# Lightning attention and mixture of depths: the first ten groups as one chunk of 128 tokens, and expert pieces between the halves of the later groups

## The chip, the cores and the metric

The kernel runs on one core of a Trainium2 chip. Time is device time in microseconds (us) of one execution of the whole program. The engines are named as in the profile: PE (TensorE, the matrix engine), DVE (VectorE), ACT (ScalarE), POOL (GpSimd) and SP (SyncE, which here only issues transfers). A fp32 matmul is two matmul instructions with a weight load each (a transpose is one), so 16 matmuls of the code are x32 in the profile.

## The reference

Two steps with four batches of 768 tokens, 8 heads of 64 and, joined, 512 features. The first is linear attention with a decay `lam` per head; it walks over blocks with a running state. Any block length gives the same result up to rounding.

```python
for b in range(nb):                       # blocks of 64 tokens
    intra = einsum('bhic,bhjc->bhij', qb, kb) * Dmask      # Dmask[i, j] = lam**(i-j), i >= j
    intra = einsum('bhij,bhjd->bhid', intra, vb)
    inter = einsum('bhid,bhde->bhie', qb * lam_pow, kv_state)
    out[:, :, sl] = intra + inter
    kv_state = lam**block * kv_state + einsum('bhsd,bhse->bhde', kb * rev_pow, vb)
```

The second is a mixture of depths: each batch's 128 tokens with the highest gate score go through a small network, and the result is added to their rows.

```python
scores = einsum('bsd,d->bs', x, w_gate)
for b in range(B):
    top_idx = argpartition(-scores[b], capacity)[:capacity]        # 128 of 768
    xe = x[b, top_idx]
    ye = maximum(xe @ w1, 0.0) @ w2                                # 512 -> 1024 -> 512
    out[b, top_idx] = xe + sigmoid(scores[b, top_idx])[:, None] * ye
```

## The kernel before, in words

The work is cut into 24 groups `g` of 128 tokens, all 8 heads, six groups to a batch. One loop over `g` runs from -1 to 23, and its order is written out by hand: the program's order on each engine is the order of the calls. Iteration `g` prepares group `g+1` and finishes group `g`.

A group is computed as two chunks of 64 tokens, `c = 0, 1`, with states `n = 2g + c`. Heads come in pairs: `hp` is the pair, `hh` the head in it. Every product is a 64x64 quarter of the array (`quarters()` lists 16 of them), placed on rows and columns 0 to 63 or 64 to 127.

- `transposes(g, name)`: q or k, four 128x128 transposes into a PSUM bank (`m` in the profile; four banks go round), copied to SBUF by ACT as `qT` or `kT`.
- `queries_decayed(g)`: POOL multiplies `qT` by powers of lam, giving `qs`. `keys_decayed(g)`: `kd`, by ACT in eight instructions for the first nine groups, then by POOL in one.
- `state_products(g)`: `kd` times v, into the right half of the PSUM tile `su`; `next_state(n)`: DVE adds the decayed state to it; `decay_state(n)`: POOL decays a state. So a group has the chain state, decay, state, decay over DVE and POOL.
- `scores(g)`: k times q into the left half of `su`; `masked(g)`: DVE multiplies by the decay mask, giving `p`.
- `from_states(g)`: `qs` times the two states, into the PSUM tile `o_`; `from_scores(g)`: `p` times v, added to it. Between them `settle(g)`, a tiny DVE copy `seen` that reads `o_`, so that the second waits until the first has arrived.
- `outputs(g)`: ACT copies `o_` to the output tile `x_b` in three instructions; `store(g)`: SP writes it to DRAM; `gate_scores(g)`: DVE's product `xg` of `x_b` with the gate weights, summed to a score per token.

The ranks follow a few groups later: `row(g)` (PE transposes the scores, ACT copies them), `compare(g)` (DVE compares every score with all of its batch, giving `beat`, `table`, `ranks`), `column_sums(g)` (PE sums the tables, DVE subtracts), and after a batch's last group `find(b)` (DVE, six `hit` instructions), `tokens(b)` (PE, with two DVE steps) and `fetch(b)` (POOL's indirect transfer of the 128 chosen rows; `take` is both). The network of a batch is 17 pieces: `gate` (four transposes of the rows), eight `hidden` (eight instructions of 128x128 each), eight `back` (two of 128x512). `products(n)` runs the next `n` pieces. `flush()` runs what goes after: `weigh` and `finish` (DVE's `y`, then POOL's indirect write).

SP's queue holds the loads and the stores in the order of the calls: three loads of 256 KB for one group, then the store of the group before. `AHEAD` is the number of load buffers, `ahead(g)` how many groups ahead loads are asked for (4 at first); from iteration `W0` on, the network's weights are loaded.

In iterations before `START = 9` the loop has no pieces: transposes of `g+1`, `row` and sums, `from_states(g)`, `settle(g)`, `gate_scores(g-1)`, `compare(g-2)`, `state_products(g+1)`, `from_scores(g)`, `scores(g+1)`, `outputs(g)`, the two states, `masked(g+1)`. From 9 on, three pieces with the rank work stand ahead of the transposes; then the rest follows in the same order, with `gate_scores(g)` at the end.

Of the kernel before, what the change touches and what calls it, by code (L numbers as in the profile page):

```python
# [17 lines left out]
def kernel(  # L18
# [29 lines left out]
    AHEAD = 10  # L48
    W0 = 9
    START = 9  # L50
# [52 lines left out]
    ident2 = const.tile([128, C], FP32, name="ident2")  # L103
    nc.vector.tensor_tensor(out=ident2[:], in0=ident[:, :C], in1=ident[:, C:], op=ALU.add)
    zero = const.tile([128, C], FP32, name="zero")
    nc.vector.memset(zero[:], 0.0)

    mask = const.tile([128, 2, NHP, C], FP32, name="mask")
    for hh in range(2):
        for hp in range(NHP):  # L110
            h = 2 * hp + hh
            nc.vector.tensor_tensor_scan(
                out=mask[:, hh, hp, :], data0=lam_b[:, h : h + 1].broadcast_to([128, C]),
                data1=ident2[:], initial=0.0, op0=ALU.mult, op1=ALU.add,
            )
    kpow = const.tile([128, NHP, 2], FP32, name="kpow")
    nc.vector.tensor_copy(kpow[:].rearrange("p a b -> p b a"), mask[:, :, :, C - 1])
# [3 lines left out]
    qpow = const.tile([128, NHP, 2, C], FP32, name="qpow")  # L121
    for hp in range(NHP):
        for c in range(2):
            nc.vector.tensor_tensor_scan(
                out=qpow[:, hp, c, :], data0=lam_p[:, hp : hp + 1].broadcast_to([128, C]),
                data1=zero[:], initial=1.0, op0=ALU.mult, op1=ALU.add,
            )
    decay = const.tile([128, NHP, D], FP32, name="decay")
    nc.vector.tensor_copy(decay[:], qpow[:, :, 0, C - 1 : C].broadcast_to([128, NHP, D]))
# [14 lines left out]
    states, decayed = {}, {}  # L144
# [6 lines left out]

    def keys_decayed(g):
        if g >= NG:
            return
        kd = att.tile([128, H, D], FP32, name="kd", bufs=2)
        if g < START:
            for h in range(H):
                nc.scalar.activation(  # L158
                    kd[:, h, :], loaded[g][0][:, h, :], AF.Copy,
                    scale=kpow[:, h // 2, h % 2 : h % 2 + 1],  # L160
                )
            kds[g] = kd
            return
        nc.gpsimd.tensor_tensor(  # L164
            out=kd[:], in0=loaded[g][0][:],
            in1=kpow[:].rearrange("p a b -> p (a b)").unsqueeze(2).broadcast_to([128, H, D]),
            op=ALU.mult,
        )
        kds[g] = kd
# [14 lines left out]
    def queries_decayed(g):  # L184
        if g >= NG:
            return
        qs = att.tile([128, NHP, L], FP32, name="qs")
        nc.gpsimd.tensor_tensor(  # L188
            out=qs[:], in0=qTs[g][:], in1=qpow[:].rearrange("p a c i -> p a (c i)"), op=ALU.mult
        )  # L190
        qss[g] = qs

    def scores(g):
        if g >= NG:
            return
        qT, kT = qTs.pop(g), kTs.pop(g)
        for hp, hh, c in quarters():
# [5 lines left out]
    def masked(g):  # L203
        if g >= NG:
            return
        p = att.tile([128, 2, NHP, C], FP32, name="p")
        nc.vector.tensor_tensor(
            out=p[:].rearrange("p a b i -> p a (b i)"), in0=su[:, :, : NHP * C],
# [4 lines left out]
    def state_products(g):  # L213
        if g >= NG:
            return
        vn, kd = loaded[g][2], kds.pop(g)
        for hp, hh, c in quarters():
# [9 lines left out]
    def decay_state(n):  # L227
        if n // 2 >= NG or n % (2 * NT) == 0 or n % (2 * NT) == 2 * NT - 1:
            return
        t = att.tile([128, NHP, D], FP32, name="decayed", bufs=2)  # L230
        nc.gpsimd.tensor_tensor(out=t[:], in0=states[n][:], in1=decay[:], op=ALU.mult)  # L231
        decayed[n] = t

    def next_state(n):
        if n // 2 >= NG or n % (2 * NT) == 2 * NT - 1:
            return
        new = att.tile([128, NHP, D], FP32, name="state", bufs=8)
        u = su[:, n % 2, NHP * C :].rearrange("p (b e) -> p b e", e=D)
# [4 lines left out]
        states[n + 1] = new  # L243

    def from_states(g):
        qs = qss.pop(g)
        for hp, hh, c in quarters():
# [11 lines left out]
    def from_scores(g):  # L259
        p, vn = ps_.pop(g), loaded.pop(g)[2]  # L260
        for hp, hh, c in quarters():
            nc.tensor.matmul(  # L262
                o_[half[hh ^ c], hh, hp * D : (hp + 1) * D],
                lhsT=p[half[c], hh, hp, :], rhs=vn[half[c], 2 * hp + hh, :],
# [12 lines left out]
    def outputs(g):  # L277
# [4 lines left out]
        x_b = x_bs[b]  # L282
        po = [o_[:, hh, : NHP * D].rearrange("p (b e) -> p b e", e=D) for hh in range(2)]
# [11 lines left out]
    def gate_scores(g):  # L295
        b, t = divmod(g, NT)
        xg = mod.tile([128, HD], FP32, name="xg")
        nc.vector.tensor_tensor_reduce(  # L298
# [191 lines left out]

    def constants():
        nc.gpsimd.memset(lead[:], TINY)
# [52 lines left out]
    def early(g):  # L545
        return g < START

    def second(g):
        next_state(2 * g + 1)
        decay_state(2 * g + 2)  # L550

    for g in range(-1, NG):
# [5 lines left out]
        if early(g):  # L558
            transposes(g + 1, "qT")
            transposes(g + 1, "kT")  # L560
            if NGR:
                row(g - 2)
                column_sums(g - 3)
        else:
            products(1)
            if NGR:
                column_sums(g - 3)
                row(g - 2)
                if ends(g - 4) and (g - 4) // NT > 0:
                    take((g - 4) // NT)  # L570
                compare(g - 2)
                if ends(g - 3):
                    find((g - 3) // NT)
            products(1 + (not ends(g - 6)))
            if ends(g - 6):
                for i in range(NGR):
                    pieces.extend(expert((g - 6) // NT, i))
                products(1)
            transposes(g + 1, "qT")
# [83 lines left out]
```

## Time and profile before

| | us |
|---|---|
| runs, median of 3 | 204.72 (204.28 to 207.6) |
| profiled execution | 202.72 |
| its span, first to last instruction | 200.9 |
| PE busy | 157.3 (78%), 3580 matmul instructions |
| DVE, POOL, ACT busy | 103.7, 90.1, 88.0 |
| mean granted clock of TensorE | 0.955 |

The durations below are of the profiled execution; 1.8 us of its time lie outside of the span, and the median of the runs is 2.0 above it. Busy time is that of an engine's instructions; a matmul's end is modelled. "Idle before" is the time that an engine stood still ahead of a group of instructions, with the instruction that released it; "issue" there means that nothing in the profile released it. The granted clock is the share of 2.4 GHz; its lower level is 1.2 GHz, 0.5.

### The profile page before, as it was taken

The page shows a single profiled execution, that of the slowest core. Times are in us where ns is not written, and L with a number is a line of the kernel's source. Part 1 is how long each engine was busy: PE and PEld are TensorE (multiplying, and loading weights), DVE is VectorE, ACT ScalarE, POOL GpSimd, SP SyncE. Part 2 cuts the span into 40 slices and gives each one's busy share as a digit, 9 for nine tenths or more (in the row PEclk, how much of TensorE's full clock was granted, in tenths as well). Part 3 has the DMA queues.
Part 4 walks back from the last instruction along what each step waited for, and adds up shares of the span by engine and source line. Part 5 has one row for each costly group of instructions (what it writes and reads, how often), then busy time and mean ns, then how long its engine had stood idle before and what let it go on. Part 6 is the DMA issues. An engine that isn't in the chain of part 4 may idle for free.

```text
span 200.9 us, 8297 instructions
## 1 busy us (share of the span) xinstructions
PE 157.3 (78%) x3580; PEld 129.4 (64%) x3580; DVE 103.7 (52%) x376; ACT 88.0 (44%) x257; POOL 90.1 (45%) x99
## 2 busy tenths in 40 slices
PE   0597765973977768795969995998999859998990
PEld 0496655962975657695836774998666649748730
DVE  2636663763678676575435658274766566001001
ACT  0968887696452443453324352354424441103200
POOL 3165555053585956357337837355596120102001
PEclk9999997999798899999999999799999996999999
DMA  3999999599688989999989998911022120101001
GB/s 107 229 224 247 247 226 206 116 224 218 129 186 196 324 194 295 253 242 263 300 197 250 260 224 190 264 64 54 7 68 92 55 77 33 52 0 55 0 0 52
DMA packets 82500, 32.26 MB, mean 161 GB/s; under 512 B 75680, under 2 KB 77728, under 8 KB 82464
## 3 DMA queue, kind: packets, MB, share of 16 engines
q1 hardware_dynamic: 81536, 29.37, 62.1%
q0 software_dynamic: 640, 2.10, 3.0%
q8 instruction: 28, 0.46, 1.0%
q10 hardware_dynamic: 288, 0.27, 0.4%
q14 instruction: 8, 0.07, 0.1%
HBM read 24.38 MB, written 7.34 MB: 158 GB/s over the span
## 4 chain that ended last, share of the span: by engine, by line
PE 49%; issue 18%; DVE 14%; POOL 8%; DMA 5%; ACT 3%; POOLq 1%; SPq 0%; DVEq 0%; ACTq 0%
PE m L450 11%; PE m L177 10%; PE m L462 7%; PE o L251 5%; PE o L262 5%; PE su L198 5%; PE su L221 5%; DVE xg L298 4%; POOL decayed L231 4%; POOL qs L188 3%; DMA qn<-in_q_dram 3%; DVE state L242 2%; DMA out_dram<-y,tok 2%; DVE y L475 1%; DVE table L339 1%
## 5 line engine op out<-in xcount | busy, mean ns | idle before, releaser
L231 POOL TENSOR_TENSOR decayed<-state,decay 128x256 f32<-128x256 f32 x40 | 34.5, 863 | 33.1 <-DVE state L242 26.9
L188 POOL TENSOR_TENSOR qs<-qT,qpow 128x512 f32<-128x512 f32 x24 | 31.1, 1294 | 34.0 <-ACT qT L181 34.0
L450 PE MATMUL m<-xsT,w_sb 128*128 128x128 f32 x256 | 36.1, 296 | 9.1 <-DVE y L475 3.8
L450 PEld LDWEIGHTS m<-xsT,w_sb 128*128 128x128 f32 x256 | 33.0, 206 | 10.5 <-DVE y L475 4.1
L242 DVE TENSOR_TENSOR state<-su,decayed 128x256 f32<-128x256 f32 x40 | 17.0, 425 | 30.8 <-PE su L198 20.8
L462 PE MATMUL m<-w_sb,hs 128*128 128x512 f32 x64 | 30.6, 605 | 0.0
L298 DVE CUSTOM_DVE_ANT_0 xg<-x_b,wg_b 128x512 f32<-128x512 f32 x24 | 25.0, 1040 | 2.0 <-ACT x_b L286 2.0
L177 PE MATMUL m<-ident,qn 128*128 128x128 f32 x96 | 17.0, 306 | 10.0 <-DMA qn<-in_q_dram 7.3
L198 PE MATMUL su<-qT,kT 64*64 64x64 f32 x768 | 17.8, 227 | 7.0 <-issue 6.9
L284 ACT COPY x_b<-o 128x256 f32<-128x256 f32 x24 | 8.9, 373 | 31.5 <-PE o L262 31.5
L251 PE MATMUL o<-state,qs 64*64 64x64 f32 x704 | 18.7, 235 | 4.5 <-issue 4.5
L177 PEld LDWEIGHTS m<-ident,qn 128*128 128x128 f32 x96 | 12.2, 155 | 14.5 <-issue 12.1
L181 ACT COPY qT<-m 128x512 f32<-128x512 f32 x24 | 14.0, 582 | 15.6 <-PE m L177 15.6
L251 PEld LDWEIGHTS o<-state,qs 64*64 64x64 f32 x704 | 14.9, 143 | 8.2 <-issue 7.7
L198 PEld LDWEIGHTS su<-qT,kT 64*64 64x64 f32 x768 | 15.2, 142 | 7.7 <-issue 7.4
L221 PE MATMUL su<-vn,kd 64*64 64x64 f32 x704 | 18.5, 231 | 1.8 <-POOL kd L164 1.7
L454 ACT ACTIVATE hs<-m 128x128 f32<-128x128 f32 x32 | 8.9, 277 | 24.3 <-PE m L450 24.2
L262 PE MATMUL o<-vn,p 64*64 64x64 f32 x768 | 17.3, 228 | 2.4 <-DVE seen L272 2.4
L479 POOL DMA_INDIRECT out_dram<-y,tok x4 | 4.6, 1158 | 30.6 <-DVE y L475 30.6
L158 ACT ACTIVATE kd<-kn,kpow 128x64 f32<-128x64 f32 x72 | 18.2, 335 | 0.2
L286 ACT COPY x_b<-o 64x256 f32<-64x256 f32 x48 | 17.6, 367 | 0.6
L221 PEld LDWEIGHTS su<-vn,kd 64*64 64x64 f32 x704 | 16.0, 145 | 2.7 <-POOL kd L164 2.0
(61 smaller groups left out, 207.5 us busy)
## 6 DMA issues: line engine op xcount, KB each, us to landing
kn<-in_k_dram SPq DMA_DIRECT2D x24, 256.0 KB, 4.5
qn<-in_q_dram SPq DMA_DIRECT2D x24, 256.0 KB, 5.2
vn<-in_v_dram SPq DMA_DIRECT2D x24, 256.0 KB, 5.6
out_dram<-x_b SPq DMA_DIRECT2D x24, 256.0 KB, 3.6
w_sb<-in_moe_w_dram SPq DMA_DIRECT2D x8, 512.0 KB, 5.5
wg_b<-in_moe_w_gate_dram ACTq DMA_DIRECT2D x1, 256.0 KB, 4.7
xs<-out_dram,tok POOLq DMA_INDIRECT x4, 4.2
out_dram<-y,tok POOLq DMA_INDIRECT x4, 3.4
```

The lines of the kernel that those rows point to most:

```text
L158: nc.scalar.activation(kd[:, h, :], loaded[g][0][:, h, :], AF.Copy, scale=kpow[:, h // 2, h % 2 : h % 2 + 1],)
L177: nc.tensor.transpose(tp[:, hp * L : (hp + 1) * L], in_=t[:, 2 * hp : 2 * hp + 2, :], identity=ident[:])
L188: nc.gpsimd.tensor_tensor(out=qs[:], in0=qTs[g][:], in1=qpow[:].rearrange("p a c i -> p a (c i)"), op=ALU.mult)
L198: nc.tensor.matmul(su[half[c], hh, hp * C : (hp + 1) * C], lhsT=kT[half[hh], hp, half[c]], rhs=qT[half[hh], hp, half[c]], start=True, stop ...
L221: nc.tensor.matmul(su[half[hh], c, NHP * C + hp * D : NHP * C + (hp + 1) * D], lhsT=kd[half[c], h, :], rhs=vn[half[c], h, :], start=True, ...
L231: nc.gpsimd.tensor_tensor(out=t[:], in0=states[n][:], in1=decay[:], op=ALU.mult)
L242: nc.vector.tensor_tensor(out=new[:], in0=u, in1=decayed.pop(n)[:], op=ALU.add)
L251: nc.tensor.matmul(o_[half[hh ^ c], hh, hp * D : (hp + 1) * D], lhsT=qs[half[hh], hp, half[c]], rhs=states[n][half[hh], hp, :], start=(hp ...
L262: nc.tensor.matmul(o_[half[hh ^ c], hh, hp * D : (hp + 1) * D], lhsT=p[half[c], hh, hp, :], rhs=vn[half[c], 2 * hp + hh, :], start=(hp == ...
L298: nc.vector.tensor_tensor_reduce(out=xg[:], in0=x_bs[b][:, t].rearrange("p a b e -> p (a b e)"), in1=wg_b[:], scale=1.0, scalar=0.0, op0=A ...
L450: nc.tensor.matmul(ph, lhsT=w1_sb[:, dc, f * 128 : (f + 1) * 128], rhs=keep["xsT"][:, dc, :], start=(dc == 0), stop=(dc == NDC - 1),)
L462: nc.tensor.matmul(py[:], lhsT=keep["hs"][:, f, :], rhs=w2_sb[:, f, :], start=(f == 0), stop=(f == NFC - 1),)
```

## The change

The first ten groups (`WIDE = 10`) are computed as one chunk of 128 tokens: `scores` is eight matmuls with 128 columns of weights and 128 moving columns, `from_states` eight with 128 columns of weights over half of the rows, `from_scores` eight with 128x128 weights and 64 moving columns, `state_products` eight over all rows. A group has one state and one decay instead of two. The state products go to a bank of their own, the scores fill all of `su`, the mask product is one of 1024 columns, `x_b` is copied by ACT in one instruction, the gate score reads `o_` in PSUM with a reordered copy of the gate weights (`wg_o`), `settle` is gone, and the keys of all groups are decayed by POOL. The constants are made for 128 tokens; `narrow_constants` takes those for 64 from them.

In the wide iterations `row(g-1)`, `compare(g-1)` and `column_sums(g-2)` come one group earlier than before, and `from_states(g+1)` stands in the iteration of group `g`, after `scores(g+1)`. In the later iterations the transposes come first, then `from_states(g)`, `settle(g)`, `state_products(g+1)` and the first state; then the pieces with the rank work and the second state; then `from_scores(g)`, `scores(g+1)`, outputs and mask. A batch's pieces begin at `ends(g - 5)` instead of `ends(g - 6)`. `AHEAD` is 8 instead of 10, and `W0` 8 instead of 9.

```diff
-    AHEAD = 10
-    W0 = 9
-    START = 9
+    AHEAD = 8
+    W0 = 8
+    WIDE = 10
...
     def scores(g):
         if g >= NG:
             return
         qT, kT = qTs.pop(g), kTs.pop(g)
+        if wide(g):
+            for hp in range(NHP):
+                for hh in range(2):
+                    nc.tensor.matmul(
+                        su[:, hh, hp * L : (hp + 1) * L], lhsT=kT[half[hh], hp, :],
+                        rhs=qT[half[hh], hp, :], start=True, stop=True, skip_group_check=True,
+                    )
+            return
         for hp, hh, c in quarters():
...
+                    nc.tensor.matmul(
+                        ub[half[hh], hp * D : (hp + 1) * D], lhsT=kd[:, h, :], rhs=vn[:, h, :],
+                        start=True, stop=True, skip_group_check=True,
+                    )
...
+                        nc.tensor.matmul(
+                            o_[:, hh, hp * D : (hp + 1) * D], lhsT=qs[half[hh], hp, :],
+                            rhs=states[2 * g][half[hh], hp, :],
+                            start=(hp == 0), stop=False, skip_group_check=True,
+                        )
...
+                    nc.tensor.matmul(
+                        o_[:, hh, hp * D : (hp + 1) * D], lhsT=p[:, hh, hp * L : (hp + 1) * L],
+                        rhs=vn[:, 2 * hp + hh, :], start=(hp == 0 and g % NT == 0), stop=True,
+                        skip_group_check=True,
+                    )
...
+        if wide(g):
+            nc.vector.tensor_tensor_reduce(
+                out=xg[:].rearrange("p (a m) -> p a m", a=2), in0=o_[:, :, : NHP * D],
+                in1=wg_o[:].rearrange("p (a m) -> p a m", a=2),
...
-        if early(g):
+        if wide(g):
+            if NGR:
+                if ends(g - 3):
+                    take((g - 3) // NT)
+                row(g - 1)
+                compare(g - 1)
+                column_sums(g - 2)
             transposes(g + 1, "qT")
             transposes(g + 1, "kT")
+            queries_decayed(g + 1)
+            if g >= 0:
+                from_scores(g)
+                outputs(g)
+                store(g)
+                gate_scores(g)
+            state_products(g + 1)
+            scores(g + 1)
+            if wide(g + 1):
+                from_states(g + 1)
...
+            next_state(2 * g + 2)
+            decay_state(2 * g + (3 if not wide(g + 1) else 4))
+            masked(g + 1)
+            second(g + 1)
+            if g == 1:
+                narrow_constants()
+            if NGR and ends(g - 2):
+                find((g - 2) // NT)
         else:
+            transposes(g + 1, "qT")
+            transposes(g + 1, "kT")
+            from_states(g)
+            settle(g)
+            queries_decayed(g + 1)
+            state_products(g + 1)
+            next_state(2 * g + 2)
+            decay_state(2 * g + 3)
+            keys_decayed(g + 2)
+            if ends(g - 5):
+                for i in range(NGR):
+                    pieces.extend(expert((g - 5) // NT, i))
             products(1)
             if NGR:
+                column_sums(g - 2)
...
+                    take((g - 3) // NT)
+                row(g - 1)
+            products(1)
+            second(g + 1)
+            if NGR:
+                compare(g - 1)
+                if ends(g - 2):
+                    find((g - 2) // NT)
+            products(1)
             from_scores(g)
+            scores(g + 1)
             outputs(g)
             store(g)
+            masked(g + 1)
             gate_scores(g)
+            flush()
```

How the instructions then stand, at three places. First PE in iteration 2, an early group, before the change (`m` is a PSUM bank, `sc` the scores of the tokens; L177 is `transposes`, L318 `row`, L251 `from_states`, L221 `state_products`, L262 `from_scores`, L198 `scores`):

```order
L177 MATMUL m_137<-ident,qn 128x128 x4
L177 MATMUL m_138<-ident,kn 128x128 x4
L318 MATMUL m_135<-ident,sc 128x128
L251 MATMUL o<-state,qs 64x64 x16
L221 MATMUL su<-vn,kd 64x64 x16
L262 MATMUL o<-vn,p 64x64 x16
L198 MATMUL su<-qT,kT 64x64 x16
```

And PE in iteration 1 of the changed kernel, from its `row` on (L401 `row`, L180 `transposes`, L324 `from_scores`, L248 `state_products`, L208 `scores`, L300 `from_states`):

```order
L401 MATMUL m_134<-ident,sc 128x128
L180 MATMUL m_135<-ident,qn 128x128 x4
L180 MATMUL m_132<-ident,kn 128x128 x4
L324 MATMUL o<-vn,p 128x64 x8
L248 MATMUL m_133<-vn,kd 64x64 x8
L208 MATMUL su<-qT,kT 128x128 x8
L300 MATMUL o<-state,qs 128x64 x8
```

64 matmuls of a quarter have become 32 wider ones, and `from_states` has moved behind `scores`, for the next group.

Second, DVE in the wide iteration 7 of the changed kernel, with what each instruction waits for (L374 is `gate_scores` with its accumulator, L289 `next_state`, L224 `masked`, L457 `find`, L472 and L474 `tokens`, L413 and L422 `compare`):

```order
L374 ISA xg,sc<-o,wg_o 128x512 [waits Activation_49]
L374 ISA sc 128x1
L289 TENSOR_TENSOR state<-m_133,decayed 128x256 [waits PE_49,Pool_49]
L224 TENSOR_TENSOR p<-su,mask_w 128x1024 [waits PE_49]
L457 TENSOR_SCALAR hit,found<-slot,ranks 128x128 [waits DVE_49]
L457 TENSOR_SCALAR hit,found<-slot,ranks 128x128 x5
L472 COPY two<-m_134 128x2 [waits PE_49]
L474 SCALAR_TENSOR_TENSOR tok_0_790<-two 128x1
```

The gate score now stands in the iteration of its own group, reads `o` and waits for ACT; `hit` stands between the mask and the token numbers.

Third, PE in a late group before the change, from the last two pieces ahead of iteration 17's transposes to two pieces of iteration 18 (L462 is `back`, L356 `column_sums`):

```order
L462 MATMUL m_138<-w_sb,hs 128x512 x2
L177 MATMUL m_136<-ident,qn 128x128 x4
L177 MATMUL m_137<-ident,kn 128x128 x4
L251 MATMUL o<-state,qs 64x64 x16
L221 MATMUL su<-vn,kd 64x64 x16
L262 MATMUL o<-vn,p 64x64 x16
L198 MATMUL su<-qT,kT 64x64 x16
L462 MATMUL m_138<-w_sb,hs 128x512
L356 LDWEIGHTS table
L356 MATMUL m_135<-ones,table 128x1
L318 MATMUL m_136<-ident,sc 128x128
L462 MATMUL m_138<-w_sb,hs 128x512 x2
```

And PE in a late iteration of the changed kernel (L311 `from_states`, L257 `state_products`, L545 `back`, L439 `column_sums`, L401 `row`, L331 `from_scores`, L214 `scores`):

```order
L180 MATMUL m_135<-ident,qn 128x128 x4
L180 MATMUL m_132<-ident,kn 128x128 x4
L311 MATMUL o<-state,qs 64x64 x16
L257 MATMUL su<-vn,kd 64x64 x16
L545 MATMUL m_134<-w_sb,hs 128x512
L439 LDWEIGHTS table
L439 MATMUL m_133<-ones,table 128x1
L401 MATMUL m_135<-ident,sc 128x128
L545 MATMUL m_134<-w_sb,hs 128x512
L331 MATMUL o<-vn,p 64x64 x16
L214 MATMUL su<-qT,kT 64x64 x16
```

The pieces and the rank work have moved from ahead of the transposes to between `state_products` and `from_scores`.

## Rows read from the trace of the kernel before

**Rows 1.** Windows by stage: length, busy us (instructions) by engine, granted clock, DMA share, GB/s

```profile
15.70:67.00 51.30, 37.20 (x1220) 33.70 (x1219) 30.83 (x109) 34.53 (x109) 26.51 (x28) 0.90 0.91 201
67.00:162.00 95.00, 80.84 (x1994) 65.99 (x1992) 56.88 (x198) 39.19 (x104) 53.58 (x52) 0.98 0.72 186
162.00:200.90 38.90, 30.88 (x173) 22.06 (x172) 9.33 (x40) 5.70 (x22) 4.37 (x4) 0.94 0.10 34
```

**Rows 2.** Timeline: start, length, engine, line, operation, tiles, idle before

```profile
15.69 1.19 SPq L290 DMA_DIRECT2D out_dram<-x_b  x1
...
67.03 0.36 SPq L290 DMA_DIRECT2D out_dram<-x_b  x1
...
161.31 0.74 ACT L286 COPY x_b<-o 64x256 f32<-64x256 f32 x2
...
171.41 0.96 POOL L408 DMA_INDIRECT xs<-out_dram,tok  x1 [6.45 <-DVE tok L391]
...
180.17 0.60 PE L421 MATMUL m<-ident,xs 128*128 128x128 f32 x4
```

**Rows 3.** Waits of PE in S1, 15.7 to 67: total, times, longest

```profile
PE o L251 <- issue: 4.5, 3, 1.7
PE su L198 <- issue: 4.2, 2, 3.3
PE m L177 <- issue: 2.5, 1, 2.5
```

**Rows 4.** Chain of work that ended last, 14 to 20 us

```profile
14.46 0.47 PE su L198 x32
14.93 1.03 PE m L177 x8
...
16.45 1.51 issue
...
18.87 0.55 PE o L262 x32
```

**Rows 5.** Windows between three gaps of PE, columns as in rows 1

```profile
17.90:22.50 4.60, 3.43 (x127) 3.05 (x127) 2.96 (x6) 3.72 (x13) 2.72 (x3) 1.00 1.11 266
22.70:27.50 4.80, 3.38 (x127) 3.00 (x127) 3.45 (x9) 4.15 (x15) 2.31 (x3) 1.00 1.02 228
```

**Rows 6.** DMA queues of the whole run: packets, MB, share of 16 engines

```profile
q8 instruction: 28, 0.46, 1.0%
```

**Rows 7.** Chain of work that ended last, 160 us to the end

```profile
162.09 0.69 DVE xg L298
...
162.79 0.66 DVE y L475
...
170.68 2.79 PE m L450 x24
173.46 6.88 PE m L462 x16
```

**Rows 8.** Groups of instructions: shape, count, busy us, mean ns, idle before

```profile
L207 DVE TENSOR_TENSOR p<-su,mask 128x512 f32<-128x512 f32 x24 | 16.3, 681 | 0.0
...
L181 ACT COPY qT<-m 128x512 f32<-128x512 f32 x24 | 14.0, 582 | 15.6 <-PE m L177 15.6
...
L374 DVE TENSOR_SCALAR_CACHE_REDUCE hit<-slot,ranks 128x128 bf16<-128x128 f32 x24 | 6.7, 341 | 0.0
```

**Rows 9.** Waits of PE in S2, 67 to 162

```profile
PE su L198 <- issue: 2.7, 2, 2.0
PE o L262 <- DVE seen L272: 2.4, 2, 1.8
PE m L450 <- issue: 2.3, 1, 2.3
PE m L450 <- DVE y L475: 2.3, 1, 2.3
```

**Rows 10.** DMA issues: median us from issue to landing

```profile
xs<-out_dram,tok POOLq DMA_INDIRECT x4, 4.2
```

More of the change, by code (lines that the diff above doesn't have):

```diff
@@ L143 @@
     qTs, qss, kTs, kds, ps_ = {}, {}, {}, {}, {}
-    states, decayed = {}, {}
+    states, decayed, us = {}, {}, {}
     x_bs, scs = {}, {}
@@ L216, in state_products @@
         vn, kd = loaded[g][2], kds.pop(g)
+        if wide(g):
+            if g % NT == NT - 1:
+                return
+            ub = bank()
+            us[g] = ub
+            for hp in range(NHP):
+                for hh in range(2):
+                    h = 2 * hp + hh
+                    nc.tensor.matmul(
+                        ub[half[hh], hp * D : (hp + 1) * D], lhsT=kd[:, h, :], rhs=vn[:, h, :],
+                        start=True, stop=True, skip_group_check=True,
+                    )
+            return
         for hp, hh, c in quarters():
@@ L282, in outputs @@
         x_b = x_bs[b]
+        if wide(g):
+            nc.scalar.copy(
+                out=x_b[:, t].rearrange("p b a e -> p a b e"),
+                in_=o_[:, :, : NHP * D].rearrange("p a (b e) -> p a b e", e=D),
+            )
+            return
         po = [o_[:, hh, : NHP * D].rearrange("p (b e) -> p b e", e=D) for hh in range(2)]
@@ L489 @@
     in_cap = const.tile([128, 1], FP32, name="in_cap")
+    wg_o = const.tile([128, HD], FP32, name="wg_o")
     def constants():
+        nc.scalar.copy(
+            out=wg_o[:].rearrange("p (a b e) -> p a b e", a=2, e=D),
+            in_=wg_b[:].rearrange("p (b a e) -> p a b e", a=2, e=D),
+        )
         nc.gpsimd.memset(lead[:], TINY)
@@ L565 @@
             products(1)
             if NGR:
[L567 to L571, printed above, removed]
-                if ends(g - 3):
[L573 to L578, printed above, removed]
@@ L579 @@
-            transposes(g + 1, "qT")
-            transposes(g + 1, "kT")
-            if NGR and ends(g - 4) and (g - 4) // NT == 0:
-                take(0)
-        if g >= 0:
-            from_states(g)
-            settle(g)
-            if early(g):
-                if g > 0:
-                    gate_scores(g - 1)
-                if NGR:
-                    compare(g - 2)
-        else:
-            constants()
-        queries_decayed(g + 1)
-        state_products(g + 1)
-        if g >= 0:
+                column_sums(g - 2)
@@ L603 @@
-        keys_decayed(g + 2)
-        masked(g + 1)
-        second(g + 1)
-        if NGR and early(g) and ends(g - 3):
-            find((g - 3) // NT)
-        if g >= 0 and not early(g + 1):
+            masked(g + 1)
             gate_scores(g)
-        flush()
+            flush()
     if NGR:
-        column_sums(NG - 3)
-        row(NG - 2)
-        compare(NG - 2)
-        products(2)
+        column_sums(NG - 2)
+        products(3)
         row(NG - 1)
         compare(NG - 1)
-        column_sums(NG - 2)
```

133 lines of the change are left out of this document (84 added, 49 removed).

## The prediction, made before the changed kernel ran

> **What bounds the kernel now.** I read the page first: in the chain of waits that ended last, matrix engine (PE) work leads, and second comes "issue", time in which the engine waited for nothing that the profile shows. Then I cut the span into stages and read the busy times of each alone [rows 1]; the cuts are moments when an output tile `x_b` is complete: group 0 at 15.7 us, group 9 at 67.0, group 23 at 162.05 [rows 2]. So S0 is 15.7 us, S1 (nine groups) 51.3, S2 (fourteen groups, with expert pieces) 95.0, S3 (the rest) 38.9; their sum is the span of 200.9.
>
> In every stage PE is the busiest engine: 37.2 of 51.3 us in S1, 80.8 of 95.0 in S2, 30.9 of 38.9 in S3 [rows 1]. DMA moves 0.91 of what it can in S1, but no engine waits for a load there. What PE loses in S1 is 14 us of idle time and a clock that is granted at 0.90 on average, so about 10 us at the lower level of 1.2 GHz, which costs about half of that.
>
> Most of that idle time has one regular cause. The waits of PE in S1 put 11.2 us, in six gaps, down to "issue" [rows 3], and the chain shows one of them, 1.51 us, in the middle of a run of equal matmuls [rows 4]. Between this gap and the next, and between that and the third, PE runs exactly 127 matmuls and 127 weight loads [rows 5]: with the waits among them, some 256 instructions. One DMA queue is named "instruction" and has 28 transfers, 0.46 MB, so 16 KB each [rows 6]; PE's 7160 instructions are 28 such blocks. I read the gaps as PE waiting for its next block. In S1 a block is used up in about 3.4 us of PE work and arrives every 4.8 [rows 5].
>
> **The change, part by part.** *Wide groups, PE.* The quarter products of a group are four families of 16 matmuls of 64x64, two passes each; one family takes 0.47 to 0.55 us [rows 4], some 15 ns per pass, because four quarters of the array work side by side. In ten groups they become four families of 8 on wider operands, also two passes. No row shows these shapes. The nearest rows are 128x128 passes of the expert, 2.79 us for 24, so 116 ns each, and 107 when nothing interrupts; 512 columns take 6.88/16 = 430 ns, four times as much [rows 7], so a pass streams 64 columns in about 54 ns. `from_scores` now holds 128 rows and 128 columns of weights and streams 64 columns: between 54 ns (the stream) and 162 ns (a 107 ns load that nothing hides, and the stream). I take 109 ns, that a load as large as the expert's sets the pace: 16 x 0.109 = 1.74 us. `scores` streams 128 columns over half of the rows, and two of them lie side by side in the array: 55 ns if they run together as the quarters do, 109 if not; I take 0.87 us. `from_states` likewise 0.87 (0.45 to 1.74), `state_products` 0.47 (to 0.93). Together 3.95 us instead of about 2.05, four families at 0.47 to 0.55. The transposes stay at 0.95 (1.03 in the row [rows 4]), rows and column sums at 0.23. So PE's work per group goes from 3.3 to 5.1 us.
>
> The Trainium skill bears on the largest of these. "TensorE: Matmul & The Clock Gate", section Back-to-back issue gap, gives about 60 cycles for any matmul of 1 to 64 columns; by that a `from_scores` family would cost 16 x 25 ns = 0.4 us, an estimate from that page. The same page's section on LDWEIGHTS has a load cost that grows with the columns of the weights, 107 ns for 128. The page so stands on both sides, and its first rule is the second rival below.
>
> *Wide groups, the loop through the other engines.* `from_states(g+1)` may not write `o_` before `gate_scores(g)` has read it, and the order of the new kernel shows that reader waiting for ACT's copy of the same tile. So after the last `from_scores` matmul come its end (0.29 from dispatch to ACT's start, estimated from a matmul's 0.23 and a semaphore), the `x_b` copy of 512 columns (0.58 as the equal copy of `qT` [rows 8]), `xg` 0.69 with its accumulator 0.76 [rows 7], twice 0.05 for semaphores, `from_states` 0.87, `row` and sums 0.23, transposes 0.95, `from_scores` 1.74: 5.53 us. PE's own 5.1 fit inside. VectorE (DVE) has, beside `xg`, a mask product of 1024 columns (at most twice the 0.68 of 512 [rows 8], so 1.2 to 1.36 us), one state and the ranks: below 4 us and so below the loop. GpSimd (POOL) gets the decayed keys, 1.0, and loses one decay, 0.9; at 3.2 us it has room. ACT loses eight copies and two of its three `x_b` copies, which costs nothing, since it had not been late.
>
> S1 is then eight periods of 5.5, one of 4.5 at the start of the second batch (no `from_states`), and one stall: `find(0)` stands behind `masked(8)` on DVE, and PE's `tokens` of the next iteration wait for six `hit` instructions of 6.7/24 = 0.28 us [rows 8], with the whole next group queued behind them: +2.5. In all 8 x 5.5 + 4.5 + 2.5 = 51.0 against 51.3: **no gain in S1**. The instruction gaps go, since a group now has about 150 instructions and a block lasts 9 us, longer than the 4.8 in which one arrives; but the dearer matmuls take that time. S0 has the same matmuls at the lower clock, on the way to the first copy: +0.7 (between -0.7, if the keys on POOL come earlier, and +2).
>
> *S2.* Pieces move between `state_products` and `from_scores`. What goes are waits for DVE: 2.4 us for `seen` and part of the 2.3 for `y` [rows 9]; `settle` now has two pieces ahead of its reader, and the chain state, decay, state runs behind pieces as before. The expert starts one group earlier, so the third batch's first five `hidden` pieces fall into S2: 5 x 8 x 0.116 = +4.65. Work is 80.8 less 1.7 for the stretch at the lower clock (0.98 over 95 us [rows 1], 3.4 us of it), plus 4.65: 83.8. New idle time: the instruction gaps stay at about 5 (2.7 and 2.3 [rows 9]), as the groups here have their old number of instructions; I add 2.5, 1.3 of it at the border, where group 10 needs both half states in a row. S2 = 91.3 (88 to 96), against 95.0. Weights: the first are asked for at iteration 8 and used at 10, at least 11 us later, which hides 1 MB at S1's 201 GB/s [rows 1]; uncovered it would cost up to 5.
>
> *S3.* Eight plus three pieces are left instead of sixteen. The last fetch of rows was issued at 171.41, 9.4 us after `x_b`, and PE came to the last `gate` at 180.17, 18.1 after it, held by pieces [rows 2]. Expert 2's `y` and weighing (0.66 in the chain's row [rows 7], 1.9 together) and one `compare` (1.0) no longer stand ahead of it on DVE; the fetch goes out 6.5 us after `x_b` and lands 4.2 later [rows 10]: `gate` at +11. PE's own pieces (3 x 0.93 + 8 x 0.86 and the ranks) end at +9.5, so the fetch is what is late next. S3 = 38.9 - 7 = 31.9 (31 to 34).
>
> Sum: 16.4 + 51.0 + 91.3 + 31.9 = 190.6 of span. The profiled execution took 202.72 with its 200.9, so 192.4; the median of the runs, 204.72, is 2.0 above it: **194.4 us**.
>
> **Rivals.** *Cheap wide products.* If a pass costs what its stream does, `from_scores` is 0.87 and `from_states` 0.45: the loop is 4.2, S1 about 40, the time 194.4 - 11 = 183.4. For it: quarters show loads running beside streams [rows 4]. Against: in all rows with 128 columns of weights the stream was as long, so none shows such a load hidden behind a shorter one.
>
> *The gaps are not blocks of instructions.* Where the gaps hang on the busy DMA and not on the count of instructions, S1 keeps them: six of 1.5 us or more, +9: 203, no change. The Trainium skill says something near it: "Runtime: NRT & Kernel Launch", section Instruction fetch mechanics, has blocks of 256 instructions and calls the cost of crossing one mostly hidden. The trace agrees on the 256 and not on the hiding, 1.51 us in the row [rows 4]. By the page, with fewer instructions nothing would come back.
>
> *Slower: halves that don't run together.* If matmuls on the upper and lower half of the rows follow each other, `scores` and `from_states` are 1.74 each and `state_products` 0.93: 6.9 to 7.3 us per group and S1 66, so 194.4 + 15.5 = 210. It decides from 1.2 us per group upward. For it: each streams a full 128 columns of the array; against: the quarters, which share rows and columns, run together.
>
> *S2 keeps its waits.* If S2's fourteen groups stay at 6.8 us and take the five pieces on top, S2 = 99.6: 203.
>
> **How the numbers follow.** The forecast has 0.50, cheap products 0.15, gaps that stay 0.13, S2 as it was 0.12, serial halves 0.10. The range goes from the second case to just above the two at 203: 183 to 205, and leaves out serial halves and tails. A measurement of this kernel can tell about 2%, so 200.6 and 208.8 are the bounds: faster 0.70 (the first two and a little of the cases at 203), same 0.22, slower 0.08.
>
> **What would show it.** In the changed profile: x32 groups of 64x64 gone before 60 us; `from_scores` at 1.7 us for 16, `scores` at 0.9; `x_b` complete every 5.5 us in S1; no "issue" gap over 1 us there and a granted clock near 1.00; 23 instruction blocks; in S2 no wait of `from_scores` for `seen`; the last `gate` 11 us after the last `x_b`, waiting for the fetch. The prediction is wrong where a pass of 128x64 weights costs far from 109 ns, or where S2's idle time doesn't fall from 14 us to about 8.

## The result, and the profile after

The changed kernel took **192.97 us** (median of 4 runs, 191.5 to 194.87); the kernel before took 204.5 in the same comparison. The ratio is 0.944 (95% interval 0.935 to 0.954). 194.4 had been forecast, in a range of 183 to 205. Ratios here leave out executions that a lower clock disturbed, so a ratio and the quotient of two medians can differ a little.

The profiled execution is the slowest of the four: 194.87, with a span of 193.1. Its stages are cut as those of before [rows 1], at the moments when `x_b` is complete: group 0 at 17.0, group 9 at 71.54, group 23 at 162.15. These are the windows of the changed kernel, with the same columns:

```profile
0.00:17.00 17.00, 9.04 (x82) 8.03 (x82) 8.26 (x21) 4.63 (x7) 7.88 (x18) 1.00 1.04 189
17.00:71.54 54.54, 52.84 (x676) 50.08 (x679) 31.50 (x96) 18.96 (x41) 26.43 (x26) 0.94 0.92 214
71.54:162.15 90.61, 86.75 (x2072) 70.26 (x2064) 58.56 (x203) 40.50 (x110) 48.35 (x52) 1.00 0.71 179
162.15:193.10 30.95, 24.25 (x128) 15.39 (x127) 6.68 (x29) 3.88 (x15) 3.17 (x3) 0.96 0.10 34
```

| stage | before | forecast | after |
|---|---|---|---|
| S0 | 15.7 | 16.4 | 17.0 |
| S1 | 51.3 | 51.0 | 54.5 |
| S2 | 95.0 | 91.3 | 90.6 |
| S3 | 38.9 | 31.9 | 30.95 |

So the time came from S2 and S3, 12.3 us together; the ten wide groups did not bring any. In S1 PE is now busy for 52.8 of 54.5 us, where it had been busy for 37.2 of 51.3: its idle time is gone, and its work has taken the place. Of S1, 3.3 us is the clock (0.94 on the mean of 54.54 us, 0.06 x 2 x 54.54 = 6.5 us at the lower level, half of it lost); without that it is 51.2.

The chain of work of the changed kernel in one wide iteration (start, length, what):

```profile
18.99 0.25 PE m L401
19.25 0.87 PE m L180 x8
20.12 1.73 PE o L324 x16
21.85 0.62 PE m L248 x16
22.47 1.09 PE su L208 x16
23.56 0.90 PE o L300 x16
24.46 0.25 PE m L401
```

PE runs from one family to the next without a wait, and 5.47 us later stands at the same place (the families add up to 5.46). `from_scores` (L324) is 1.73 where 1.74 had been forecast. The timeline of the changed kernel at the one point where PE could have had to wait, `from_states` (L300) behind the reader of `o`:

```profile
22.51 0.69 DVE L374 CUSTOM_DVE_ANT_0 xg<-o,wg_o 128x512 f32<-128x512 f32 x1 [2.38 <-ACT x_b L353]
...
23.13 0.08 DVE L374 DVE_READ_ACCUMULATOR2_ANT sc<- 128x1 f32 x1
...
23.32 1.00 PEld L300 LDWEIGHTS o<-state,qs 64*128 64x128 f32 x16
```

The score is complete at 23.21 (23.13 and 0.08), and the first load of `from_states` starts at 23.32. The loop through ACT and DVE is hardly longer than PE's own work: in all of S1 PE waited once for it, 0.4 us.

Copies of `x_b` by ACT in the changed kernel show how regular this is, and where it is not (groups 0, 7, 8, 9):

```profile
16.42 0.58 ACT L353 COPY x_b<-o 128x512 f32<-128x512 f32 x1 [2.09 <-PE o L324]
...
54.76 0.58 ACT L353 COPY x_b<-o 128x512 f32<-128x512 f32 x1 [1.04 <-PE o L324]
63.59 0.58 ACT L353 COPY x_b<-o 128x512 f32<-128x512 f32 x1 [2.29 <-PE o L324]
70.96 0.58 ACT L353 COPY x_b<-o 128x512 f32<-128x512 f32 x1 [1.04 <-PE o L324]
```

Seven periods of 5.48 on the mean (5.10 to 5.63; the shortest is the one forecast at 4.5), then 8.83 and 7.37. The chain of the changed kernel there:

```profile
57.70 1.60 DVE hit L457 x12
...
60.57 2.98 PE o L324 x16
63.55 1.05 PE m L248 x16
64.60 2.01 PE su L208 x16
```

PE waits for `hit` with the next group queued behind `tokens`; then the clock is at its lower level from 60.8 to 67.6, and the same families take 2.98 instead of 1.73 and 2.01 instead of 1.09.

The instruction queue of the page, and the waits of PE in S1 and in S2 of the changed kernel (S1's three rows are all that the view has); last, a wait of S2 in the kernel before (L533 and L450 are `hidden` after and before):

```profile
q8 instruction: 23, 0.38, 0.8%
```

```profile
PE m L467 <- DVE hit L457: 0.7, 1, 0.7
PE o L300 <- DVE sc L374: 0.4, 1, 0.4
PE o L324 <- DVE p L224: 0.2, 1, 0.2
```

```profile
PE su L214 <- issue: 1.2, 2, 0.9
PE m L533 <- ACT xsT L509: 1.0, 2, 0.5
PE o L311 <- ACT x_b L361: 0.9, 1, 0.9
PE m L533 <- issue: 0.5, 1, 0.5
```

```profile
PE m L450 <- ACT hs L454: 2.3, 1, 2.3
```

No "issue" gap is left in S1, where there were 11.2 us of them [rows 3]; in S2 the waits for `seen` and `y` [rows 9] and for `hs` are gone, and the "issue" gaps are 1.7 us instead of 5.0. In S3 of the changed kernel the last fetch and the last `gate` stand so:

```profile
168.75 0.99 POOL L491 DMA_INDIRECT xs<-out_dram,tok  x1 [14.85 <-DVE tok L474]
...
172.24 0.45 PEld L504 LDWEIGHTS m<-ident,xs 128*128 128x128 f32 x4 [0.58 <-DMA xs<-out_dram,tok]
```

6.6 us after the last `x_b` and 10.1 after it (forecast: 6.5 and 11), where it had been 9.4 and 18.1 [rows 2].

### The profile page after: what moved, and what is told of

It reads as the page before. It is cut to its first block, busy times and chain, and to the rows that moved or that the text cites. A ratio compares the mean times of both kernels' runs of the same rounds, so it can differ in the third digit from the quotient of the medians.

```text
span 193.1 us, 6937 instructions
## 1 busy us (share of the span) xinstructions
PE 172.9 (90%) x2940; PEld 143.8 (74%) x2940; DVE 105.0 (54%) x349; ACT 68.0 (35%) x170; POOL 85.8 (44%) x98
## 4 chain that ended last, share of the span: by engine, by line
PE 73%; DVE 9%; issue 9%; DMA 4%; ACT 2%; POOL 1%; POOLq 1%; DVEq 0%
PE m L533 12%; PE m L180 10%; PE m L545 10%; PE o L324 10%; PE su L208 5%; PE o L331 5%; PE o L311 4%; PE o L300 4%; PE su L214 4%; PE su L257 3%; PE m L248 3%; PE m L401 2%; DMA out_dram<-y,tok 2%; DVE p L224 2%; DMA lam_b<-in_lam_dram 2%
## 5 line engine op out<-in xcount | busy, mean ns | idle before, releaser
L533 PE MATMUL m<-xsT,w_sb 128*128 128x128 f32 x256 | 32.2, 280 | 2.1 <-ACT xsT L509 1.6
L533 PEld LDWEIGHTS m<-xsT,w_sb 128*128 128x128 f32 x256 | 29.8, 192 | 3.5 <-ACT xsT L509 2.3
L545 PE MATMUL m<-w_sb,hs 128*128 128x512 f32 x64 | 30.9, 605 | 0.0
L180 PE MATMUL m<-ident,qn 128*128 128x128 f32 x96 | 16.3, 295 | 7.2 <-DMA qn<-in_q_dram 7.2
L324 PE MATMUL o<-vn,p 128*128 128x64 f32 x160 | 20.4, 284 | 0.9 <-DVE p L224 0.9
L324 PEld LDWEIGHTS o<-vn,p 128*128 128x128 f32 x160 | 19.8, 202 | 1.3 <-DVE p L224 1.0
L270 POOL TENSOR_TENSOR decayed<-state,decay 128x256 f32<-128x256 f32 x23 | 16.7, 726 | 3.8 <-DVE state L289 2.9
L374 DVE CUSTOM_DVE_ANT_0 xg<-o,wg_o 128x512 f32<-128x512 f32 x10 | 6.9, 692 | 20.6 <-ACT x_b L353 20.6
L545 PEld LDWEIGHTS m<-w_sb,hs 128*128 128x128 f32 x64 | 11.1, 193 | 8.1 <-issue 7.7
L180 PEld LDWEIGHTS m<-ident,qn 128*128 128x128 f32 x96 | 10.8, 147 | 8.3 <-issue 7.4
L230 DVE TENSOR_TENSOR p<-su,mask 128x512 f32<-128x512 f32 x14 | 9.7, 691 | 11.4 <-PE su L214 11.3
L180 PE MATMUL m<-ident,kn 128*128 128x128 f32 x96 | 14.9, 279 | 0.0
L167 POOL TENSOR_TENSOR kd<-kn,kpow 128x512 f32<-128x512 f32 x14 | 14.6, 1040 | 0.0
L184 ACT COPY kT<-m 128x512 f32<-128x512 f32 x24 | 14.2, 592 | 0.3 <-PE m L180 0.3
L289 DVE TENSOR_TENSOR state<-su,decayed 128x256 f32<-128x256 f32 x23 | 9.7, 423 | 7.0 <-POOL decayed L270 3.8
L208 PE MATMUL su<-qT,kT 64*128 64x128 f32 x160 | 13.5, 315 | 0.0
```

Source lines behind the costliest of these rows:

```text
L167: nc.gpsimd.tensor_tensor(out=kd[:], in0=loaded[g][0][:], in1=pw[:].rearrange("p a b -> p (a b)").unsqueeze(2).broadcast_to([128, H, D]), ...
L180: nc.tensor.transpose(tp[:, hp * L : (hp + 1) * L], in_=t[:, 2 * hp : 2 * hp + 2, :], identity=ident[:])
L184: nc.scalar.copy(out=dst[:].rearrange("p a i -> p (a i)"), in_=tp[:])
L208: nc.tensor.matmul(su[:, hh, hp * L : (hp + 1) * L], lhsT=kT[half[hh], hp, :], rhs=qT[half[hh], hp, :], start=True, stop=True, skip_group_ ...
L230: nc.vector.tensor_tensor(out=p[:, :, : NHP * C], in0=su[:, :, : NHP * C], in1=mask[:].rearrange("p a b i -> p a (b i)"), op=ALU.mult,)
L270: nc.gpsimd.tensor_tensor(out=t[:], in0=states[n][:], in1=(decay_w if wide(g) else decay)[:], op=ALU.mult)
```

## The experiments

Each was compared with the kernel before on its own chip. Times are medians; the ratio to the kernel before stands with its interval.

**One part alone.** *late_order_only*: the kernel before with the changed kernel's later iterations, all groups narrow; they begin at 10, as there.

```diff
-    AHEAD = 10
-    W0 = 9
-    START = 9
+    AHEAD = 8
+    W0 = 8
+    START = 10
...
-        else:
-            products(1)
...
+        else:
+            transposes(g + 1, "qT")
+            transposes(g + 1, "kT")
+            from_states(g)
+            settle(g)
...
```

> All groups stay narrow; only the later iterations (from 10 on) have the new order, with batches' pieces one group earlier. Theory A (the gain is in the later order, the wide groups bring none): S0 and S1 as before, 15.7 + 51.3, then 90.6 + 31.0 as in the changed kernel, span 188.6, time 190 to 194. Rival B (the wide groups bring at least half of the gain, for instance because fewer instructions ahead keep the later ones on time): 198 or more.

189.17 us (188.03 to 190.8), ratio 0.948 (0.924 to 0.972). Its windows by the same cuts:

```profile
0.00:15.56 15.56, 8.38 (x199) 7.63 (x200) 6.60 (x31) 8.62 (x24) 5.60 (x17) 1.00 0.99 188
15.56:65.23 49.67, 36.54 (x1218) 32.81 (x1217) 31.46 (x109) 36.19 (x118) 26.35 (x27) 0.91 0.93 220
65.23:155.41 90.18, 87.09 (x2041) 70.63 (x2040) 59.94 (x209) 40.80 (x111) 49.54 (x52) 0.99 0.75 192
155.41:186.40 30.99, 24.25 (x128) 15.43 (x127) 6.68 (x29) 3.88 (x14) 3.16 (x3) 1.00 0.10 34
```

S2 and S3 are those of the changed kernel, S0 and S1 nearly those of before, "issue" gaps in S1 included:

```profile
PE su L198 <- issue: 4.7, 2, 3.6
PE o L251 <- issue: 3.2, 3, 1.4
PE m L177 <- issue: 2.7, 2, 2.2
```

Theory A holds: the later order earns the whole gain. On another chip the same kernel, *late_order_again*:

> All groups narrow with the new later order once more (189.17 on another chip), beside a kernel with wide groups on the same chip. Theory A (the wide groups earn nothing): 188 to 193, within 2 per cent of the changed kernel's two medians, 192.97 and 193.37; if the wide groups earn something, 195 or more.

191.05 us (188.31 to 193.38), ratio 0.928 (0.920 to 0.936). So the wide groups seem even to cost time: the runs that enter the ratios took 188.0 to 190.8 us in the narrow kernel (seven) and 191.0 to 193.6 in the changed one (five). With a difference below 2%, and on several chips, that is not shown for certain.

*wide_only* is the other part: the changed kernel with the old later order.

```diff
         else:
-            transposes(g + 1, "qT")
...
-            if ends(g - 5):
+            products(1)
...
+            if ends(g - 6):
```

> The first ten groups wide as in the changed kernel; the later iterations in the old order, with pieces ahead of the transposes and batches' pieces one group later. Theory A: 17.0 + 51 to 54.5 + 95 + 38.9, so 202 to 207, no gain over the kernel before. Rival B: 193 to 198.

204.33 us, ratio 1.020 (0.987 to 1.053): no gain. S2 and S3 of its profile:

```profile
74.52:168.03 93.51, 81.28 (x2025) 65.96 (x2017) 54.95 (x192) 38.99 (x102) 51.86 (x50) 0.98 0.68 166
168.03:206.80 38.77, 30.74 (x173) 21.98 (x172) 9.33 (x40) 5.64 (x22) 4.38 (x4) 0.94 0.10 34
```

**The split order, or the earlier begin of a batch's pieces?** *pieces_later* is the changed kernel with `ends(g - 6)` in place of `ends(g - 5)`; *old_order_pieces_earlier* is wide_only with `ends(g - 5)`.

> The changed kernel, but a batch's pieces begin one group later, as in the kernel before; the split order stays. Theory A1 (the split order alone earns the gain: in S2 and S3 the matrix engine is busy nearly throughout, so moved pieces only move time): S2 shorter by 4.7 to 6.6, S3 longer by as much, the time within 2 us of the changed kernel. Rival F (the earlier begin is what earns S3's 8 us): S3 back at 38 to 39 and S2 not shorter, 198 to 201.

197.15 us (191.96 to 199.06; too scattered for a ratio). Three `hidden` pieces move to S3, fewer than I had taken when I wrote 4.7 to 6.6 us. S3 of its profile is 33.95 instead of 30.95, but S2 stays at 90.47; its "issue" gaps are 3.4 us together, 1.7 in the changed kernel. By its trace neither expectation holds.

> Wide early groups, the later iterations in the old order (pieces ahead of the transposes) but with a batch's pieces begun one group earlier, as in the changed kernel. Theory A1 (the split order earns S2's gain, since it takes the waits for seen, state and y away; an earlier begin alone puts work into iterations that still wait): S2 no shorter than 91, S3 3 us shorter than before's 38.9 or as it was, 200 to 205, as the run with the old order that had 204.3. Rival F (the earlier begin earns most of S3): S3 31 to 33 with S2 as in the old order, 195 to 199.

204.12 us, ratio 0.994 (0.990 to 0.998), as wide_only. In its profile S3 is 33.1, as rival F has it, but S2 is 100.4 at a clock of 0.94 (93.5 at 0.98 in wide_only): what leaves S3 comes back in S2. So an earlier begin alone earns nothing, and the split order is what matters: 204.3 and 204.1 in the old order, 197.2 and 193.0 in the new one. The runs take the new order as a whole; what the pieces between the halves, the transposes ahead and the earlier rank work each earn, they don't show. What the earlier begin adds to the split order, up to 4 us, lies within pieces_later's scatter.

**What the gaps hang on.** *narrow_few_loads*: the kernel before, groups 3 to 9 computed from the tiles of groups 0 to 2 (so of other inputs).

```diff
     def load(g):
+        if 3 <= g < 10:
+            loaded[g] = first[g % 3]
+            return
...
```

> The kernel before, in which groups 3 to 9 use the tiles of groups 0 to 2 again, so that S1 has nearly no loads (the output is of other inputs); the number of matrix instructions is the same. Theory D (the gaps of the matrix engine come about every 256 instructions, and are long because the block's transfer stands among busy queues): six gaps fall from 11.2 us to below 5, S1 from 51.3 to 43 to 46. Rival E (a crossing costs 1.5 to 2 us whatever the queues do): gaps stay at 9 to 11 and S1 at 50 to 52.

198.01 us in one run. S1 and the waits of PE in it (in this kernel L204 is `scores`, L183 `transposes`, L257 `from_states`, L268 `from_scores`):

```profile
15.61:62.19 46.58, 35.66 (x1220) 31.43 (x1219) 29.94 (x110) 34.00 (x109) 27.57 (x28) 0.97 0.43 111
```

```profile
PE su L204 <- issue: 4.6, 3, 1.9
PE m L183 <- issue: 1.7, 1, 1.7
...
PE o L257 <- issue: 1.0, 2, 0.6
...
PE o L268 <- issue: 0.4, 1, 0.4
```

With the DMA share down from 0.91 to 0.43 the gaps fall from 11.2 to 7.7 us, and S1 to 46.6; a part of that is the clock, 0.97 instead of 0.90. The gaps lie between theory D (below 5) and rival E (9 to 11): full queues lengthen them, and they are there without full queues too.

*alternate* makes groups 3, 5, 7 and 9 narrow and leaves the queues full:

```diff
-        return g < WIDE
+        return g in (-1, 0, 1, 2, 4, 6, 8)
```

> Groups 0, 1, 2, 4, 6, 8 wide, 3, 5, 7, 9 narrow, the rest as in the changed kernel (with token numbers behind the matrix work of iteration 8 and rank constants one iteration later). Theory A (the gaps depend on how many matrix instructions fall in a stretch of time: a wide and a narrow group together have about 400 in 9 us, a block of 256 per 5.7 us, longer than the 4.8 in which one arrives): no gap over 1 us in S1, a period of 4.5 to 5.0 on the mean of the mixed groups, S1 45 to 48, 184 to 188 us. Rival G (the narrow groups pause anyway, or the loads of 1 MB per group bound the period at 5.5): S1 50 or more, 189 to 193.

196.94 us, ratio 0.966 (0.961 to 0.972): a miss, slower than either forecast. No "issue" gap is left, but in three places `row`, at the head of a wide iteration, waited for a gate score that a narrow iteration makes late:

```profile
PE m L401 <- DVE sc L381: 5.1, 3, 2.2
```

*alternate_row_later* moves `row` and `column_sums` behind `scores` and `compare` behind the mask.

> The alternating kernel, in which the wide iterations run row and column_sums behind the matrix work of scores, and compare behind the mask. The waits of row for the gate score there (5.1 us in three) were a mishap of my order and hid what the theory said. Theory A (gaps by the number of instructions in a stretch): again no gap without a releaser in S1, and with those waits gone S1 is 40 to 45 instead of 49.6 (part of that is the clock, 0.86 on average in S1 there, which falls behind the stalls), 185 to 190 us. Rival G (the loads bound the period): S1 48 or more, 192 or more.

190.9 us, ratio 0.937 (0.931 to 0.944). Windows and waits of PE, from 15.4 to 62 us, short of the border to group 10:

```profile
15.40:62.00 46.60, 42.25 (x872) 38.08 (x870) 31.61 (x93) 20.25 (x45) 28.31 (x34) 1.00 0.96 217
```

```profile
PE o L324 <- DVE p L224: 0.6, 1, 0.6
PE m L248 <- issue: 0.6, 1, 0.6
PE o L331 <- DVE seen L341: 0.6, 1, 0.6
PE o L300 <- ACT x_b L361: 0.5, 2, 0.2
```

With the DMA at 0.96, more than before, one gap of 0.6 is left. So the number of PE instructions in a stretch of its work decides whether the gaps come in S1: 872 matmuls in 42.25 us of work here, 1220 in 37.20 before [rows 1], or 6.2 and 3.9 us for each 128 matmuls with their 128 loads, where a block arrived every 4.8 [rows 5]. A mean does not settle every case: S2 has 5.2 us before and 5.4 in the changed kernel, and gaps in both. The groups from 2 to 8 come every 5.09 us on the mean, but S1 was 49.4 (16.24 to 65.64), as rival G has it and not 40 to 45. No wait of PE in it is for a load; at the border, where group 10 follows, `state_products` and `scores` wait for the half states:

```profile
PE su L257 <- DVE state L289: 2.5, 1, 2.5
PE su L214 <- DVE state L289: 1.7, 1, 1.7
```

**The stall for `hit`.** *tokens_later* puts the first batch's `tokens` and `fetch` one iteration later (`ends(g - 4)` for `ends(g - 3)` in the wide branch).

> The changed kernel with the first batch's token numbers and fetch one iteration later, so that matrix work of group 8 is not queued behind the six hit instructions. Theory A (the stall of 3.3 us in S1 is theirs, and the stretch at the lower clock that begins behind it, 3.4 us more in the profiled run, follows from it): 3.3 to 6.7 us less than the changed kernel, 186 to 190. Rival C (another wait, or the loads of 1 MB per group, takes the place): within 1 us of the changed kernel.

191.45 us (191.25 to 192.34), ratio 0.958 (0.940 to 0.976). Its `x_b` of group 9 is complete at 66.41 instead of 71.54, and the clock does not fall there. But the fetch now takes 7 us and the `gate` of iteration 10 waits for it:

```profile
PE m L504 <- DMA xs<-out_dram,tok: 1.2, 1, 1.2
```

Group 10 is complete at 75.91, in the changed kernel at 79.75, of which the clock is 3.3: most of the stall of two microseconds is given back at once, and what the profiled execution gains is the clock. That is less than theory A wanted; where the clock did not fall, rival C is near (the changed kernel's five runs with a mean clock of 0.98 or more took 191.0 to 193.6).

*wide_two_fixes* puts `take(0)` behind `from_states(9)` in iteration 8, and makes the constants of the ranks in iteration 0.

```diff
-                if ends(g - 3):
-                    take((g - 3) // NT)
...
             if wide(g + 1):
                 from_states(g + 1)
+            if NGR and ends(g - 3):
+                take((g - 3) // NT)
...
+            if g == 0:
+                rank_constants()
```

> The changed kernel with two moves: the first batch's token numbers stand behind the matrix work of iteration 8, and the rank constants are made one iteration later. Theory A (the stall for hit is 3.3 us and is given back only where the fetch comes late, which it does not here; the first mask product waits 1 us for constants): 3 to 4.5 us less than the changed kernel, 187 to 189.5. Rival C (the fetch still comes late for the gate, or the loads bound the wide groups): less than 1.5 us.

190.56 us (189.76 to 191.17), ratio 0.938 (0.930 to 0.947); 2.8 less than the changed kernel's median on the same chip, but by the ratios (0.938 and 0.944) only about 1, as rival C has it. S0 falls from 16.92 to 15.79 by the constants. Group 10 is complete at 75.82 again: the token numbers on DVE now hold up the mask of group 9, and iteration 10 waits for states. A second hold-up lies in the chain there, one DVE instruction of `compare`:

```profile
64.38 3.29 DVE L427 SCALAR_TENSOR_TENSOR ranks<-same,prev 128x1 f32<-128x1 f32 x1
```

Its median in this trace is 0.31 us. `xg` of group 9, whose input was ready at 66.36, starts only behind it, at 67.66, and the states follow `xg`. Why it took so long the runs do not show. On that chip *changed_again* is the changed kernel once more:

> The changed kernel once more, for a trace without the stretch at the lower clock at 61 us, and as what the others of this call are compared with. Where the S1 term of the forecast holds, S1 is 51.1 (54.5 less the 3.4 that the clock took) and the time 191 to 193.5; where the 3.4 us come from something else than the clock, S1 stays at 54.

193.37 us (191.03 to 195.82), ratio 0.944 (0.930 to 0.957). Its trace, too, has the fall of the clock behind the stall:

```profile
55.27:73.06 17.79, 16.66 (x182) 15.63 (x186) 8.20 (x33) 3.95 (x8) 7.38 (x8) 0.71 0.98 259
```

S1 is 56.1; 0.29 x 17.79 = 5.2 of that is the clock, and 51.0 is left, nearly the 51.2 of the first trace. The same stall stands in the traces of pieces_later, wide_only and old_order_pieces_earlier, and in all three the clock falls to its lower level behind it, between 58 and 60 us; in those of tokens_later and wide_two_fixes, where `tokens` is moved, it is at 1.00 from 40 to 80 us. It does not fall in every execution: of the changed kernel's eight runs three have a mean clock of 0.974 to 0.976, as the two profiled ones, and five 0.984 to 1.0.

*narrow_tokens_mid* moves `take(0)` behind `scores` in the narrow kernel (late_order_only):

> All groups narrow with the new later order (the run that had 189.17), and the first batch's token numbers behind the matrix work of iteration 9. Theory A (the wait for hit, 1.0 us there, is the only part of the stall that reaches the end): 188 to 188.5, and still 2 us or more under the changed kernel. Rival: the late fetch gives it back, 189 or more.

192.96 us, ratio 0.948 (0.938 to 0.958), 3.8 more than late_order_only's 189.17 in an earlier comparison on the same chip: the rival. Group 10 is complete only at 79.34, in late_order_only at 73.3. The waits of PE between 65 and 79.5:

```profile
PE su L221 <- POOL kd L164: 2.2, 1, 2.2
PE m L421 <- DMA xs<-out_dram,tok: 1.4, 1, 1.4
```

The `gate` waits for the later fetch, and `state_products` for keys on POOL, the queue on which that fetch now stands. A part of the 6 us is the clock, 0.61 from 70 to 75 us and 0.71 from 75 to 80.

## Why the prediction was right, point by point

- **Total and signs: right**, and stage by stage: S2 3.7 forecast and 4.4 measured, S3 7 and 7.95, no gain in S1. late_order_only and wide_only show the split by themselves: the one has all of the gain, the other none. That the total came as near as 1.4 us is in part luck: the profiled span was 2.5 above the forecast one, while the median of the runs, taken as 2.0 above the profiled execution, was 1.9 below it.
- **`from_scores` at the pace of a 128-column load: right**, 1.73 for 1.74. The cheap rival (0.87) fell with that, and with it 183. The Trainium skill gives its 60 cycles for up to 64 columns ("TensorE: Matmul & The Clock Gate", section Back-to-back issue gap) as the gap of an isolated matmul, and says there that in a stream of weight loads and matmuls both set the spacing. The prediction read it as a rule for any matmul, 0.4 us by its estimate, and called it the second rival, where the first is meant; the 1.73 measured is four times that. The page's load cost for 128 columns, P/1.2 or 107 ns (section LDWEIGHTS), agrees with the 108 of a pass. **`scores` and `state_products` were mis-sized**: 1.09 for 0.87, 0.62 for 0.47; `from_states` was 0.90 for 0.87, the transposes 0.87 for 0.95. PE's own work is 5.46 for 5.1.
- **The loop as what binds S1: half right.** 5.53 was forecast and 5.48 measured, but the trace shows PE with next to no wait: its own sum, larger than I took it, has caught up with the loop.
- **The gaps as blocks of 256 instructions: right.** 23 blocks; no gap in S1; and with alternate_row_later they stay away under a fuller DMA. The rival in which they hang on the busy DMA is refuted as the cause; narrow_few_loads shows DMA only making them longer.
- **Serial halves: refuted.** `scores` would have been 1.74.
- **The stall at `find(0)`: 2.1 for 2.5** (8.83 less 5.48 and less the 1.25 that `from_scores` takes longer at the lower clock), but the fall of the clock behind it, 3.3 and 5.2 us in the two traces, was not in my sum. That is most of the 3.5 by which S1, and more than the 2.5 by which the profiled span, lay above the forecast. The traces of tokens_later and wide_two_fixes do not have it, and the mean clock of their eight runs is 0.984 or more.
- **S0: 1.3 instead of 0.7**, for another reason than given: the rank constants stood on DVE ahead of the first mask. wide_two_fixes takes 1.1 of it away.
- **S2's parts: the sum was right by luck, since two terms were off against each other.** I had 83.8 of work and 7.5 idle; it is 86.75 and 3.9. Of the 2.95 of work too few, about 1 is `scores`, of which one group more lies within the cuts; `from_states` (9.70 us in both kernels), `from_scores` (9.69 and 9.73) and `state_products` (8.85 and 8.86) are no dearer, and what the rest is the runs do not show. The instruction gaps, which I left at 5, fell to 1.7. They fall with the new later order, wide groups or not: 5.0 in the kernel before and in wide_only, 5.1 in old_order_pieces_earlier, but 0.7 and 0.6 in the two traces with narrow groups, 1.7 and 0.8 in the two of the changed kernel. By which step, with as many instructions per group, the runs do not show.
- **S3: right in mechanism**: the fetch and PE's last pieces end together, at 172. PE's load for the last `gate` waits 0.58 for the fetch.

Open: what the earlier begin of the pieces is worth (0 to 4 us), and why group 10 comes at 75.8 to 75.9 us in tokens_later and wide_two_fixes and, less the clock, at 76.1 to 76.4 in the changed kernel, where narrow groups had it at 73.3 in one trace and 76.7 in the other.

## What to carry to other kernels

Ahead of replacing many small matmuls by fewer wide ones, add up what PE will then be busy for: here 11 us of idle time went, and the dearer passes took all of it, so that half of the change earned nothing. Work that fills waits is worth most where the waits are: putting pieces between a producer and its reader took away waits for DVE and ACT, while beginning the same pieces earlier in the old order did nothing. A short stall of PE can cost more than its length, since the clock may fall behind it, as it did in some executions here; look for the stall ahead of a slow stretch.

## What the hardware showed that I had not expected

- One fp32 pass with 128x128 weights and 64 moving columns is 1.73/16 = 108 ns; with 128 columns of weights over 64 rows and 128 moving columns 68 ns, with 64 moving columns 56 ns, with 64 columns of weights over 128 rows 39 ns; a 64x64 quarter among its kind 15 ns.
- The clock fell to 1.2 GHz behind a stall in which PE did two microseconds of nothing but a few `tokens` passes, in all five traces of kernels with wide groups that have this stall, and stayed at 2.4 GHz through S1 in the two traces where `tokens` was moved. By their mean clocks, five of the changed kernel's eight runs had little or nothing of it.
